# Three staging tiles, in place of two, for the output rows of an attention and SiLU layer kernel

## The chip, the cores and the metric

The kernel runs on one core of a Trainium2 chip. The metric is the device time of one execution in microseconds (us); lower is better. Beside it stands the profile of one execution. It gives the span from the first to the last instruction, every engine's instructions, and which instruction or transfer ended each wait.

## The reference, cut to what matters

The input is q, k and v with 8 batches, 8 heads, 576 positions and 64 channels. Four heads attend in a sliding window of 32 positions, the other four in a dilated window (every fourth position of 128). The result, laid out as 4608 tokens of 512 channels, goes through two dense layers with a SiLU between them:

```python
x = attn_out.transpose(0, 2, 1, 3).reshape(B * S, H * D)   # 4608 x 512
h = x @ w_in                                               # 4608 x 2048
g = h * (1.0 / (1.0 + np.exp(-h)))
out = (g @ w_out).astype(np.float32)                       # 4608 x 512
```

## The kernel before, in words

The tokens are cut into ten groups: groups 0 and 1 of 256 tokens, groups 2 to 9 of 512. For each group a first layer writes `gT` (L975 and L984 for most groups), and a second layer multiplies it by `w_out` and writes finished rows to `out`. The attention of the eight batches (score matmuls L692, exponentials L701 and L705, masks L711, products with v L738, normalisation L741 and L742) is woven between the layers' matmuls. A planner in the kernel's Python decides this order when the program is built, from its own costs and due times, and writes out one fixed order of instructions for each engine. Each engine then runs its list strictly in that order. The planner knows nothing of the staging tiles of the output.

**The second layer.** Groups 0 and 1 use `layer2`: for each block of 128 tokens ScalarE copies a finished 128x512 result out of PSUM into a staging tile `ob` (L1138) and issues its write to HBM from its own queue (L1139). Groups 2 to 9 use `layer2_fast`, which computes two blocks of 128 tokens at once with seven half-size products in place of eight. One call of it for a group has two such pairs (`tb` = 0 and 1), and a pair has two staging tiles, `ob_{g}_{tb}_0` and `ob_{g}_{tb}_1`, 128x512 in float32 each. The seven steps of a pair, n = 0 to 6, each have 8 matmuls (L1209):

- n = 0, 1 and 2: ScalarE copies the half-width result to a temporary in the buffers called `nat` (L1229).
- n = 3: VectorE adds a temporary and writes one half of the first staging tile (L1236).
- n = 4: VectorE writes one half of the second staging tile (L1236).
- n = 5: VectorE writes the other half of the first staging tile, which is then written to HBM (L1241).
- n = 6: ScalarE copies the other half of the second staging tile (L1239), which is then written to HBM (L1241).

Steps 0, 2, 4 and 6 use one PSUM bank, steps 1, 3 and 5 a second. So the matmuls of n = 5 wait until VectorE has read what n = 3 left, and those of n = 6 until VectorE has read what n = 4 left:

```python
if n > 4:
    (nc.sync if g >= BYSP else nc.scalar).dma_start(out=out[row : row + P], in_=ob)
```

The writes of groups 2 to 6 are issued from ScalarE's queue, those of groups 7 to 9 (`BYSP = 7`) from SP's.

**The staging tiles.** They come from the pool `o32`, which has two buffers for each tag. The tag `ob` thus has two, the tag `th` (results of a tanh in the first groups) has two others. Tiles take the buffers of a tag in turn. The first instruction that writes into a buffer waits until the HBM write of the tile that had the buffer before has landed. Counted through the program, the tiles are number 0 to 3 (groups 0 and 1) and then four for each group, so `ob_3_1_0` and `ob_3_1_1` are tiles 10 and 11, `ob_4_0_0` and `ob_4_0_1` are 12 and 13, `ob_4_1_0` and `ob_4_1_1` are 14 and 15, and `ob_5_0_0` and `ob_5_0_1` are 16 and 17. With two buffers tile k waits for the write of tile k - 2.

Of the kernel before, what the change touches and what calls it, by code (L numbers as in the profile page):

```python
# [10 lines left out]
F32 = mybir.dt.float32  # L11
# [5 lines left out]
def kernel(  # L17
# [11 lines left out]
    DM, DFF = moe_w_in.shape  # L29
    P = 128  # L30
# [41 lines left out]
    cpool = ctx.enter_context(tc.tile_pool(name="const", bufs=1))  # L72
    gtp = ctx.enter_context(tc.tile_pool(name="gtp", bufs=2))
    o32 = ctx.enter_context(tc.tile_pool(name="o32", bufs=2))
    dram = ctx.enter_context(tc.tile_pool(name="dram", bufs=1, space=bass.MemoryType.DRAM))
    ps_h = ctx.enter_context(tc.tile_pool(name="ps_h", bufs=2, space=bass.MemoryType.PSUM))
    ps_y = ctx.enter_context(tc.tile_pool(name="ps_y", bufs=1, space=bass.MemoryType.PSUM))
# [1042 lines left out]
    def layer2(g, l1s):  # L1120
        t0 = GROUPS[g][0]
        tiles = {}

        def l2(ring, tb, f4):
            if f4 == 0:
                tiles[tb] = POOLS[ring].tile([P, DM], F32, tag=ring, name=f"y_{g}_{tb}")
            y = tiles[tb]
            for f in range(4 * f4, 4 * f4 + 4):
                nc.tensor.matmul(  # L1129
                    y, gTs[g][:, f, tb * P : (tb + 1) * P], w_out16[:, f],  # L1130
                    start=(f == 0), stop=(f == NFF - 1),
                )
            if f4 < NFF // 4 - 1:
                return
            rows = out[t0 + tb * P : t0 + (tb + 1) * P]
            ob = o32.tile([P, DM], F32, tag="ob", name=f"ob_{g}_{tb}")
            yield "ACT", 0.12 + DM / 1200
            nc.scalar.copy(ob, y)  # L1138
            nc.scalar.dma_start(out=rows, in_=ob)  # L1139

        steps = []
        for tb in range(GROUPS[g][1] // P):
            four = [
                Step(
                    lambda ring, tb=tb, f4=f4: l2(ring, tb, f4), 0.8633, [],
                    l1s[4 * f4 : 4 * f4 + 4] + [AT_WOUT[f4]], ("ACT",) if f4 == 3 else (),
                )
                for f4 in range(NFF // 4)
            ]
            four[0].keep = four[-1]  # L1150
            four[0].rings = ["y", "u"]
            steps += four
        return steps
# [25 lines left out]
    def g_parts(g):  # L1179
        t = halves(gTs[g])  # L1180
        q = [[t[:, k, :, m * HT : (m + 1) * HT] for k in range(2)] for m in range(2)]
        u = works[(g + 1) % 2].rearrange("p (i c w) -> p i c w", i=3, c=KP)
        return q, [u[:, i] for i in range(3)]

    def g_sums(g, c):
        ((A11, A12), (A21, A22)), (S1, S2, S4) = g_parts(g)
        if g in ONPOOL:
            for args in ((S1, A21, A22, ALU.add), (S2, S1, A11), (S4, A12, S2), (A21, A11, A21)):
                yield "POOL", 0.2 + (c[1] - c[0]) * HT / 480
                minus(c, *args, eng=nc.gpsimd)  # L1190
            return
        yield "DVE", 2 * sum_us(c)
        minus(c, S1, A21, A22, ALU.add)
        minus(c, A21, A11, A21)
        yield "DVE", 2 * sum_us(c)
        minus(c, S2, S1, A11)
        minus(c, S4, A12, S2)

    def layer2_fast(g, even, odd, sums, n):
        t0 = GROUPS[g][0]  # L1200
        pq = {}
        obs = {}

        def product(bank, name, lhs, rhs, tb, first):
            if name:
                pq[bank] = POOLS[bank].tile([P, DM], F32, tag=bank, name=name)
            y = pq[bank][:, :DH]
            for c in range(KP):
                nc.tensor.matmul(  # L1209
                    y, lhs[:, c, tb * P : (tb + 1) * P], rhs[:, c],  # L1210
                    start=first and c == 0, stop=c == KP - 1, skip_group_check=not first,
                )
            return y

        def step(ring, tb, n, bank):
            ((A11, A12), (S3, A22)), (S1, S2, S4) = g_parts(g)
            t1, t5, u2 = temps
            name = f"y{n}_{g}_{tb}" if n < 2 else None
            lhs, rhs, first = (
                (A11, B11, True), (S1, T1, True), (S2, T2, False), (S4, B22, False),  # L1220
                (S3, B12, False), (A12, B21, True), (A22, T4, False),
            )[n]
            y = product(bank, name, lhs, rhs, tb, first)
            if n == 3:
                for m in range(2):
                    obs[tb, m] = o32.tile([P, DM], F32, tag="ob", name=f"ob_{g}_{tb}_{m}")
            if n < 3:
                yield "ACT", 0.13 + DH / 1200
                nc.scalar.copy((t1, t5, u2)[n], y)  # L1229
                return  # L1230
            row = t0 + tb * P + HT * (n in (4, 6))
            ob = obs[tb, int(n in (4, 6))]
            half = ob[:, DH:] if n in (3, 4) else ob[:, :DH]
            if n < 6:
                yield "DVE", 0.15 + DH / 960
                nc.vector.tensor_tensor(half, y, (u2, t5, t1)[n - 3], ALU.add)  # L1236
            else:
                yield "ACT", 0.13 + DH / 1200
                nc.scalar.copy(half, y)  # L1239
            if n > 4:  # L1240
                (nc.sync if g >= BYSP else nc.scalar).dma_start(out=out[row : row + P], in_=ob)  # L1241

        steps = []
        w3 = [w_steps["last", c] for c in WPARTS]
        w2 = [w_steps["sums", c] for c in WPARTS]
        k0, k1 = sum(even, []), sum(odd, [])
        for tb in range(HT // P):
            p_bank, q_bank = "yu" if (n + tb) % 2 == 0 else "uy"
            seven = []
            more = (k0, sums + w2, sums, sums, sums + w3, k1, k1)  # L1250
            after = ((), (), (0,), (1,), (2,), (3,), (4,))
            for i in range(7):
                bank = q_bank if i in (1, 3, 5) else p_bank
                seven.append(
                    Step(
                        lambda ring, tb=tb, i=i, bank=bank: step(ring, tb, i, bank), 0.878, [],
                        list(more[i]) + [seven[x] for x in after[i]],
                        ("DVE",) if i in (3, 4, 5) else ("ACT",),
                    )
                )  # L1260
            seven[0].keep, seven[1].keep = seven[6], seven[5]
            seven[0].rings, seven[1].rings = [p_bank], [q_bank]
            steps += seven
        return steps
# [25 lines left out]
    for g in range(FAST, NG):  # L1290
        own = [
            Step(
                lambda ring, g=g, c=c: g_sums(g, c), 0.0, (),
# [125 lines left out]
```

## Time and profile before

| | |
|---|---|
| time, median of 3 runs | 305.23 us (304.96 to 305.46) |
| the profiled execution: time | 305.17 us |
| its span | 303.4 us |
| mean granted clock of TensorE | 0.989 |
| TensorE matmul busy | 288.5 us (95% of the span) |
| VectorE, ScalarE, GpSimd busy | 215.2, 194.6, 97.9 us |
| HBM writes of staging tiles, ScalarE's queue | 24 of 256 KB, median 4.0 us from issue to landing |
| the same, SP's queue | 12 of 256 KB, median 2.0 us |

In a row of the timeline the first number is the start in us from the span's start, the second the length of the merged row, then come the engine, the line, the operation, and in brackets the engine's idle time before it with what ended it. PE is TensorE's matmul part, DVE VectorE, ACT ScalarE, POOL GpSimd, SP the engine that only issues transfers. Ends of matmuls are modelled: a matmul's successor may start before its end. The length of a merged row reaches from the first start to the last end, so that it may hold a stall.

### The profile page before, as it was taken

The numbers are of one execution on the slowest core, as the hardware profiler recorded it, in microseconds if no ns is written. First come the engines' busy times: TensorE is split into PE (matmuls) and PEld (weight loads), VectorE is DVE, ScalarE is ACT, GpSimd is POOL, SyncE is SP. The second block draws the span as 40 slices with busy tenths as digits, with TensorE's granted clock in tenths as the row PEclk, the third lists the DMA queues.
The fourth block names the chain that finished last, engine by engine and source line by source line (L and its number), as shares of the span: only waits on it lengthen the run. The fifth ranks groups of instructions, "written<-read, shape, count | busy, mean of one in ns | idle before, by whom it ended". The sixth has DMA issues, their size and how long they took to land.

```text
span 303.4 us, 7434 instructions
## 1 busy us (share of the span) xinstructions
PE 288.5 (95%) x2922; PEld 203.0 (67%) x2922; DVE 215.2 (71%) x598; ACT 194.6 (64%) x427; POOL 97.9 (32%) x135
## 2 busy tenths in 40 slices
PE   6779999989999999999989999999999999999995
PEld 2458765644567666666765577558647888888884
DVE  6288999889958785768654788476767686599511
ACT  7477784378687766766746675667665496388320
POOL 8764824000740060005000659700700069800000
PEclk9599999999999999999999999999999999999999
DMA  7999999999899989989958999943114401200231
GB/s 97 180 199 198 197 194 201 208 186 194 94 155 171 240 101 182 214 179 118 210 128 182 158 192 264 211 84 110 47 34 108 110 2 50 90 2 0 86 124 71
DMA packets 100106, 42.26 MB, mean 139 GB/s; under 512 B 68584, under 2 KB 95464, under 8 KB 100072
## 3 DMA queue, kind: packets, MB, share of 16 engines
q0 software_dynamic: 48528, 19.86, 54.2%
q1 hardware_dynamic: 48088, 15.64, 26.0%
q10 hardware_dynamic: 3456, 6.29, 6.2%
q8 instruction: 23, 0.38, 0.5%
q14 instruction: 11, 0.09, 0.1%
HBM read 39.81 MB, written 17.10 MB: 188 GB/s over the span
## 4 chain that ended last, share of the span: by engine, by line
PE 77%; DVE 11%; DMA 6%; ACT 3%; issue 1%; POOL 1%; ACTq 0%; DVEq 0%; POOLq 0%
PE h L975 27%; PE y L1209 27%; PE h L1077 8%; PE y L1129 4%; DMA out_dram<-ob 4%; PE av_d L738 2%; PE s L692 2%; DMA nat<-in_q_dram 2%; DVE gT L989 2%; PE av_p L738 1%; DVE probs L711 1%; DVE oD L742 1%; DVE ob L1236 1%; DVE oP L742 1%; PE xp L784 1%
## 5 line engine op out<-in xcount | busy, mean ns | idle before, releaser
L975 PE MATMUL h<-xA,w_in 128*128 128x512 f16 (+1 forms) x512 | 110.4, 352 | 1.8 <-ACT probs L705 0.9
L984 ACT ACTIVATE gT<-h 128x512 f16<-128x512 f32 x84 | 49.6, 597 | 29.0 <-PE h L975 28.6
L975 PEld LDWEIGHTS <-w_in 128*128 128x128 f16 x512 | 45.2, 97 | 32.6 <-issue 2.5
L1209 PEld LDWEIGHTS <-gT 128*128 128x128 f16 x512 | 49.0, 98 | 8.6 <-issue 1.6
L1209 PE MATMUL y<-w_out,gT 128*128 128x256 f16 x384 | 48.4, 273 | 0.1
L1209 PEld LDWEIGHTS <-work 128*128 128x128 f16 x384 | 37.0, 98 | 7.0 <-issue 1.1
L1236 DVE TENSOR_TENSOR ob<-y,nat 128x256 f32<-128x256 f32 x48 | 20.1, 422 | 25.4 <-PE y L1209 23.3
L512 POOL COPY fence<-kqT 128x1 f16<-128x1 f16 x10 | 3.9, 397 | 94.8 <-DMA kqT<-kq_s 94.8
L1209 PE MATMUL y<-w_sum,work 128*128 128x256 f16 x256 | 32.0, 273 | 0.4 <-ACT nat L1229 0.4
L738 PEld LDWEIGHTS <-probs 128*128 128x128 f16 x448 | 22.9, 98 | 13.0 <-DVE oP L742 1.7
L701 ACT ACTIVATE probs<-s 128x768 f16<-128x768 f32 (+2 forms) x31 | 24.5, 791 | 6.3 <-PE s L692 3.4
L742 DVE TENSOR_TENSOR oD<-av_d,rcps 72x256 f16<-72x256 f32 x64 | 26.9, 421 | 2.2
L1229 ACT COPY nat<-y 128x256 f32<-128x256 f32 x48 | 17.9, 384 | 10.7 <-PE y L1209 9.5
L987 ACT ACTIVATE th<-h 128x256 f32<-128x256 f32 (+1 forms) x44 | 19.2, 445 | 7.3 <-PE h L975 4.7
L989 DVE SCALAR_TENSOR_TENSOR gT<-th,h 128x256 f16<-128x256 f32 (+1 forms) x44 | 20.6, 487 | 2.2 <-ACT th L987 2.1
L741 DVE RECIPROCAL rcps<-av_d 72x4 f32<-72x4 f32 x64 | 11.1, 173 | 14.9 <-PE av_d L738 14.8
L1239 ACT COPY ob<-y 128x256 f32<-128x256 f32 x16 | 5.9, 371 | 24.2 <-PE y L1209 21.6
L705 ACT ACTIVATE probs<-s 128x288 f16<-128x288 f32 (+2 forms) x40 | 18.5, 485 | 4.6 <-ACT ob L1239 1.4
L742 DVE TENSOR_TENSOR oP<-av_p,rcps 96x256 f16<-96x256 f32 x48 | 20.2, 421 | 1.6
L711 DVE TENSOR_TENSOR probs<-probs,mask_p 128x768 f16<-128x768 f16 x21 | 12.2, 584 | 10.2 <-ACT probs L701 7.4
L1209 PE MATMUL y<-w_sum,gT 128*128 128x256 f16 x128 | 16.6, 272 | 1.0 <-DVE ob L1236 1.0
L738 PE MATMUL av_d<-vd,probs 128*128 128x65 f16 x256 | 16.5, 194 | 0.6 <-ACT probs L705 0.3
(129 smaller groups left out, 484.3 us busy)
## 6 DMA issues: line engine op xcount, KB each, us to landing
out_dram<-ob ACTq DMA_DIRECT2D x24, 256.0 KB, 4.0
out_dram<-ob SPq DMA_DIRECT2D x12, 256.0 KB, 2.0
kq_s<-in_k_dram POOLq DMA_DIRECT2D x5, 576.0 KB, 9.1
kq_s<-in_q_dram POOLq DMA_DIRECT2D x5, 576.0 KB, 12.9
vp<-in_v_dram POOLq DMA_DIRECT2D x7, 384.0 KB, 7.0
w_out<-in_moe_w_out_dram POOLq DMA_DIRECT2D x4, 512.0 KB, 10.9
vraw<-in_v_dram POOLq DMA_DIRECT2D x8, 224.0 KB, 5.4
w_in<-in_moe_w_in_dram POOLq DMA_DIRECT2D x3, 512.0 KB, 9.5
```

Of the source, the lines that this page charges most:

```text
L701: nc.scalar.activation(p2, both[:, :, :n], AF.Exp, scale=scale)
L705: nc.scalar.activation(p2[:, i], sp[i][:, :n], AF.Exp, scale=scale)
L738: nc.tensor.matmul(a[:, i, : D + 1], lhs(i), rhs(i), start=True, stop=True)
L742: nc.vector.tensor_tensor(o, a[:n, :, :D], rcp[:n, :, None].broadcast_to([n, HN, D]), ALU.mult)
L975: nc.tensor.matmul(h[:, :w], w_in16[:, c, f * P : (f + 1) * P], x_g[:, c], start=(c == 0), stop=(c == HP - 1),)
L984: nc.scalar.activation(gTs[g][:, f, :w], h[:, :w], AF.Silu, scale=2.0)
L987: nc.scalar.activation(th[:, :w], h[:, :w], AF.Tanh)
L989: nc.vector.scalar_tensor_tensor(gTs[g][:, f, :w], th[:, :w], 1.0, h[:, :w], ALU.add, ALU.mult)
L1077: nc.tensor.matmul(y, lhs[:, c, j], rhs[:, c], start=first and c == 0, stop=c == 1, skip_group_check=not first,)
L1209: nc.tensor.matmul(y, lhs[:, c, tb * P : (tb + 1) * P], rhs[:, c], start=first and c == 0, stop=c == KP - 1, skip_group_check=not first,)
L1229: nc.scalar.copy((t1, t5, u2)[n], y)
L1236: nc.vector.tensor_tensor(half, y, (u2, t5, t1)[n - 3], ALU.add)
```

## The change

The staging tiles get a pool of their own with three buffers, so that tile k takes the buffer of tile k - 3. The pool `o32` keeps the tag `th` and its two buffers. The lines of the kernel move down by one.

```diff
     o32 = ctx.enter_context(tc.tile_pool(name="o32", bufs=2))
+    obp = ctx.enter_context(tc.tile_pool(name="obp", bufs=3))
...
-            ob = o32.tile([P, DM], F32, tag="ob", name=f"ob_{g}_{tb}")
+            ob = obp.tile([P, DM], F32, tag="ob", name=f"ob_{g}_{tb}")
             yield "ACT", 0.12 + DM / 1200
             nc.scalar.copy(ob, y)
             nc.scalar.dma_start(out=rows, in_=ob)
...
             if n == 3:
                 for m in range(2):
-                    obs[tb, m] = o32.tile([P, DM], F32, tag="ob", name=f"ob_{g}_{tb}_{m}")
+                    obs[tb, m] = obp.tile([P, DM], F32, tag="ob", name=f"ob_{g}_{tb}_{m}")
```

In the built program every engine has the same instructions in the same order as before. The third buffer takes 2 KB in each partition behind the other two, and no other buffer has another address. What differs is which earlier write the first instructions on a staging tile wait for; VectorE has three fewer instructions that only wait (89 in place of 92), ScalarE two fewer (104 in place of 106).

## The prediction

> **What bounds the kernel now.** I read the page first. TensorE's matmuls fill 95% of the span, and the chain that ended last is mostly theirs; but the chain also has a share of a kind that no computation needs, the wait for the write of an output tile.
>
> ```profile
> PE 288.5 (95%) x2922; PEld 203.0 (67%) x2922; DVE 215.2 (71%) x598; ACT 194.6 (64%) x427; POOL 97.9 (32%) x135
> ...
> PE 77%; DVE 11%; DMA 6%; ACT 3%; issue 1%; POOL 1%; ACTq 0%; DVEq 0%; POOLq 0%
> ```
>
> The chain in order of time tells where that share lies. It passes through such a write twice, and nowhere else:
>
> ```profile
> 148.26 7.22 DMA out_dram<-ob
> 155.57 0.44 DVE ob L1236
> 156.05 1.03 PE y L1209 x8
> ...
> 178.66 5.77 DMA out_dram<-ob
> 184.56 0.43 DVE ob L1236
> 185.03 1.03 PE y L1209 x8
> ```
>
> A write in this chain does not mean that its 7.22 or 5.77 us are lost; only what an engine stood idle for it is. So the list of waits comes next, of all engines: VectorE waited twice for a write of `ob`, 1.3 us in all, and TensorE once for VectorE's step behind it.
>
> ```profile
> DVE ob L1236 <- DMA out_dram<-ob: 1.3, 2, 1.2
> ...
> PE y L1209 <- DVE ob L1236: 1.0, 1, 1.0
> ```
>
> Then the timeline of the two places. Counting the rows of L1236 in threes (n = 3, 4, 5 of a pair), the row at 155.57 is n = 4 of the first pair of group 4, which opens tile 13; the row at 184.56 is n = 3 of the first pair of group 5, which opens tile 16.
>
> ```profile
> 153.19 1.91 PE L1209 MATMUL y<-w_out,gT 128*128 128x256 f16 x16
> 153.45 0.42 DVE L1236 TENSOR_TENSOR ob<-y,nat 128x256 f32<-128x256 f32 x1 [0.53 <-PE y L1209]
> ...
> 155.57 0.42 DVE L1236 TENSOR_TENSOR ob<-y,nat 128x256 f32<-128x256 f32 x1 [1.19 <-DMA out_dram<-ob]
> ...
> 156.05 1.03 PE L1209 MATMUL y<-w_sum,gT 128*128 128x256 f16 x8 [0.95 <-DVE ob L1236]
> ```
>
> ```profile
> 183.88 2.19 PE L1209 MATMUL y<-w_out,gT 128*128 128x256 f16 x16
> ...
> 184.56 0.42 DVE L1236 TENSOR_TENSOR ob<-y,nat 128x256 f32<-128x256 f32 x1 [0.16 <-DMA out_dram<-ob]
> ```
>
> Last, the stretches behind them: how much idle time does TensorE have there that could swallow what is saved? The first figure after the stretch is its length, the second PE's busy time; the clock stands after POOL.
>
> ```profile
> 145.00:160.00 15.00, 13.86 (x166) 10.55 (x165) 9.48 (x26) 8.49 (x18) 0.00 (x0) 1.00 0.88 173
> 160.00:186.00 26.00, 25.46 (x258) 17.20 (x255) 19.14 (x48) 16.74 (x32) 13.42 (x17) 1.00 1.16 182
> 186.00:240.00 54.00, 54.00 (x485) 35.75 (x484) 35.89 (x101) 32.76 (x60) 15.20 (x23) 1.00 0.49 119
> 240.00:281.00 41.00, 40.79 (x373) 36.08 (x371) 31.60 (x84) 30.84 (x85) 18.96 (x20) 1.00 0.07 27
> ```
>
> Almost none: 0.54, 0.00 and 0.21 us. From 160 us on the kernel runs at TensorE's pace, and whatever TensorE gets earlier it keeps, unless a load is then late.
>
> **Up to the first stall** nothing changes. The instructions and their order are the same, every wait for a write names an older one, and before 154 us no instruction on a staging tile was released by a write. Durations and landings up to there are those of the trace.
>
> **The first stall, tile 13.** Before, it waits for tile 11, issued at 148.26 and landed 7.22 us later, at 155.48. After, it waits for tile 10. That write was issued at 147.42 (the row of L1241 ahead of the other), and the row at 153.45, which opened tile 12 and needed it then, was released by a matmul and not by a write; so it had landed by 153.45. VectorE is free at 155.57 - 1.19 = 154.38, so nothing holds the add back then. It takes 0.42 us to 154.80, and TensorE started 0.05 us after its end (156.05 against 155.57 + 0.43), so n = 6 may start at 154.85 or a little later. What is late next is TensorE itself: n = 4 and n = 5 started at 153.19, and 16 matmuls at 0.109 us (the chain has 1.75 us for 16 of this size) let the next one start at 154.94. TensorE gains 156.05 - 154.94 = **1.11 us**. The row's own idle time says 0.95, as it counts from the modelled end of a matmul that overlaps its successor by 0.16; I take the starts, since in an unbroken run of matmuls they set the pace, and keep 0.95 as the lower end. The margin between VectorE and TensorE is only 0.09 us, so about 0.1 could go.
>
> **Between the stalls** everything moves by 1.11 us with TensorE: the adds, the copies, the mask products and GpSimd's sums, which the waits show released by score matmuls (POOL nat L1026 by PE s, 4.0 us). TensorE has one other gap there, 0.40 us at 181.82 for a copy of ScalarE (L1229), which depends on matmuls alone and moves along.
>
> **The second stall, tile 16.** Before, it waits for tile 14 (issued 178.66, landed 184.43). After, it waits for tile 13, issued some 20 us earlier. VectorE was idle for 0.16 us, so the add starts that much earlier. TensorE started 0.05 us after the add; its own pace would have had it at 183.88 + 8 x 0.109 = 184.75, against 185.03, so 0.28 us were lost, of which 0.12 remain because VectorE came late from two masks (1.89 us for both). Gain: **0.16 us**; the ends are 0.12 (the idle time that the trace gives TensorE there) and 0.28.
>
> **What is now waited for instead.** Tile 17 (n = 4 at 186.42) waits for tile 14. It would be due at 186.42 - 1.27 = 185.15, and tile 14 landed at 184.43 even if its write, issued 1.1 us earlier, landed no earlier: 0.7 us to spare. In the later groups no wait with the two buffers was ended by a write, and tile k - 3 is always issued earlier than k - 2. Some of ScalarE's copies and issues now wait by name for a write that VectorE's wait covered before; each is an older write yet (for the issue of `ob_2_0_1` at 97.29 the write of 64.45), so nothing is held behind them. Five instructions that only wait are gone, 0.02 us each by their shortest rows, on queues that run ahead of their engines: nothing.
>
> **The sum.** 1.11 + 0.16 = 1.27 us off a span of 303.4, so 302.1; with the 1.77 us around it, 305.17 - 1.27 = 303.90 us. That execution is 0.06 us below the median of the runs, which gives 303.96, and I say **304.0 us**. With the lower ends (0.95 + 0.12) it is 304.2. The greatest gain that TensorE's idle time from 145 us to 281 us admits is 1.14 + 0.54 + 0.21 = 1.89, or 2.05 with the 0.16 of overlap: 303.2.
>
> **Rivals.** *The stall belongs to this execution.* Writes of 256 KB in the issue table land in 4.0 us on ScalarE's queue and 2.0 us on SP's in the median. If the write of tile 11 mostly took 6.1 us or less, there would be no wait at 154.38 and nothing to save: 305.2 us. Against it: the profiled execution lies within 0.3 us of all three timed runs, and none of them is a microsecond shorter. For it: landing times may vary where casts from GpSimd's queue fill the transfer engines, as they do around 148 us. The Trainium skill speaks for this rival: "DMA: Bandwidth & Descriptors", section "Anatomy of one DMA", fits a transfer as about 2.0 us plus its bytes over 436 GB/s, measured on GpSimd's path. An estimate from that page is 2.6 us for 256 KB, with which both waits would be empty and the time 305.2. The trace's 7.22 us differs, and I go by the trace. Chance 0.13.
>
> *The wait moves on to tile 17.* If tile 14 lands more than 0.7 us later than in the trace, n = 4 of group 5 waits for it. A landing 0.6 us beyond that margin would cost up to 0.6: 304.6 us. For it: 5.77 us is long already, and the transfer engines are full there. Against it: the write itself is issued earlier. Chance 0.07.
>
> *Slower: the writes come earlier and the loads land later.* Writes and loads share the transfer engines, and the loads of the next batch's k and q follow right after the writes at 156.7 and 157.6. The last transposing load for the scores at 176.03 is issued at 165.36 and lands within 3.9 us (the longest of its line), at 169.3; for those at 205.80 it is issued at 194.78 and lands by 198.7. So 6.8 and 7.1 us are to spare, 5.7 with TensorE 1.1 us earlier. The rival decides only from there: it is slower by over 0.2% when loads come 5.7 + 1.27 + 0.61 = 7.6 us later than now; 8.3 us, say, would give 305.2 - 1.3 + 2.6 = 306.5. No row shows such a delay, and no load is moved or enlarged. Chance 0.06, with whatever else a new program may bring.
>
> That the change does not do what it says is ruled out by the waits of the built program, which name the write three tiles back.
>
> **How the numbers follow.** Forecast 0.74, first rival 0.13, second 0.07, third 0.06. The forecast's own range is 303.5 to 304.5: from the sum half a microsecond to either side, which takes in the lower ends at 304.2 and the 0.25 us by which the runs scatter, and most of the way to the greatest gain. To hold eight in ten the range takes in the second rival and half of the first: 303.5 to 305.2. A measurement of this kernel can tell about 0.2%, 0.6 us, from no change. The forecast and the second rival at 304.6 are both faster by that: 0.81; the same: 0.13; slower: 0.06.
>
> **What would show it.** In the profile after: no wait of `ob` L1236 for `out_dram<-ob`; no gap of TensorE ahead of n = 6 near 155 us, which starts at about 154.9; the PE row near 183 us starting some 1.1 us earlier; the stretch 145 to 160 with about 0.2 us of idle PE in place of 1.14; no DMA `out_dram<-ob` in the chain before the end of the kernel. It would be wrong if the wait is gone and TensorE still starts n = 6 after 155.5, if PE shows a new wait of over half a microsecond after 157 us, or if the span falls by less than 0.6 us.

## The result and the profile after

The changed kernel takes 303.43 us in the median of six runs (302.88 to 303.73); the kernel before takes 305.35 us beside it (304.34 to 305.48). The ratio is 0.9941, with a 95% interval from 0.9925 to 0.9957: faster by 1.92 us. The forecast said faster, by 1.27 us; the median lies 0.07 us below the low end of its range. Three later comparisons, told below, gave less: 0.80, 1.23 and 0.82 us. Here and below a median is taken over all timed runs, while a ratio leaves out six executions that were slow as a whole: four of 308.4 to 309.9 us, one of 334.8 us (of the changed kernel) and one of 1636 us.

The profiled execution of the changed kernel took 302.88 us, with a span of 301.1 us. Busy times and the engines' shares of the chain that ended last:

```profile
PE 289.0 (96%) x2922; PEld 203.6 (68%) x2922; DVE 215.4 (72%) x598; ACT 194.7 (65%) x427; POOL 97.5 (32%) x135
...
PE 81%; DVE 9%; ACT 4%; DMA 2%; issue 1%; POOL 1%; ACTq 0%; POOLq 0%
```

The work of every engine is the same to within 0.6 us. The chain's share of DMA fell from 6% to 2%, and what is left is the first load; no write of an output tile is in it. In the waits of all engines VectorE's adds (L1237 now, one line further down) wait for matmuls and for ScalarE, above all in the two rows below; no row of this view names `out_dram<-ob`:

```profile
DVE ob L1237 <- PE y L1210: 18.5, 23, 4.0
DVE ob L1237 <- ACT nat L1230: 4.1, 1, 4.1
```

The 4.1 us behind ScalarE are not new: without the waits for writes, all idle time ahead of these adds is 23.9 us, against 23.7 before. One more of these adds, at 233.24, is put down to the transfer `x_s<-oD` with 0.63 us of idle time; the same add of the kernel before (235.45) has the same 0.63 us and there it is put down to a matmul, so nothing was added.

The timeline of the first place. Tile 13's add is the row at 153.45. It follows the mask product without a wait, and TensorE goes through n = 4, 5 and 6 without a gap:

```profile
152.33 1.91 PE L1210 MATMUL y<-w_out,gT 128*128 128x256 f16 x16
152.59 0.42 DVE L1237 TENSOR_TENSOR ob<-y,nat 128x256 f32<-128x256 f32 x1 [0.53 <-PE y L1210]
...
153.45 0.42 DVE L1237 TENSOR_TENSOR ob<-y,nat 128x256 f32<-128x256 f32 x1
154.08 1.04 PE L1210 MATMUL y<-w_sum,gT 128*128 128x256 f16 x8
```

The second place. Tile 16's add is the row at 182.34; tile 17's is the first of the two merged at 184.13:

```profile
181.91 1.94 PE L1210 MATMUL y<-w_out,gT 128*128 128x256 f16 x16
182.34 0.41 DVE L1237 TENSOR_TENSOR ob<-y,nat 128x256 f32<-128x256 f32 x1
184.13 0.74 DVE L1237 TENSOR_TENSOR ob<-y,nat 128x256 f32<-128x256 f32 x2
```

And the stretches (length first, then PE's busy time). In the first of them TensorE is now idle for 0.13 us in place of 1.14:

```profile
145.00:160.00 15.00, 14.87 (x165) 11.37 (x164) 9.52 (x27) 9.40 (x20) 0.00 (x0) 1.00 1.24 220
160.00:186.00 26.00, 25.59 (x256) 17.01 (x254) 20.57 (x52) 15.96 (x29) 15.34 (x20) 1.00 1.18 185
```

The span fell by 2.29 us, 1.02 more than forecast. Laying row on row tells why. The TensorE row ahead of the first place is already 0.86 us early (152.33 against 153.19), because the first load of q landed at 9.34 us in place of 10.07. At the first place the difference grows to 1.97 (n = 6 at 154.08 against 156.05), at the second to 2.22 (the next matmuls at 184.03 against 186.25), and then little is added. So this pair of profiles holds 1.11 us from the first place, 0.25 from the second, and 0.86 from a start whose connection with the change is open: the first question for the experiments.

### The profile page after: what moved, and what is told of

Its sections match the earlier page's. It is cut to its first block, busy times and chain, and to the rows that moved or that the text cites. A ratio compares the mean times of both kernels' runs of the same rounds, so it can differ in the third digit from the quotient of the medians.

```text
span 301.1 us, 7429 instructions
## 1 busy us (share of the span) xinstructions
PE 289.0 (96%) x2922; PEld 203.6 (68%) x2922; DVE 215.4 (72%) x598; ACT 194.7 (65%) x427; POOL 97.5 (32%) x135
## 4 chain that ended last, share of the span: by engine, by line
PE 81%; DVE 9%; ACT 4%; DMA 2%; issue 1%; POOL 1%; ACTq 0%; POOLq 0%
PE y L1210 30%; PE h L976 28%; PE h L1078 8%; PE y L1130 4%; PE s L693 3%; PE av_d L739 3%; DMA nat<-in_q_dram 2%; DVE gT L990 2%; PE av_p L739 2%; DVE probs L712 1%; ACT th L988 1%; DVE oP L743 1%; ACT probs L702 1%; PE xp L785 1%; DVE oD L743 1%
## 5 line engine op out<-in xcount | busy, mean ns | idle before, releaser
L1237 DVE TENSOR_TENSOR ob<-y,nat 128x256 f32<-128x256 f32 x48 | 20.1, 422 | 24.4 <-PE y L1210 18.5
L513 POOL COPY fence<-kqT 128x1 f16<-128x1 f16 x10 | 3.2, 329 | 93.2 <-DMA kqT<-kq_s 93.2
L1210 PE MATMUL y<-w_out,work 128*128 128x256 f16 x128 | 16.6, 273 | 0.0
```

The lines of the kernel that those rows point to most:

```text
L1210: nc.tensor.matmul(y, lhs[:, c, tb * P : (tb + 1) * P], rhs[:, c], start=first and c == 0, stop=c == KP - 1, skip_group_check=not first,)
```

## The experiments

Twelve runs were made, in three sets on three chips; some kernels were run more than once. The main theory is the prediction's: the gain comes from the waits for the writes of tiles 11 and 14, and is some 1.3 us. Against it stood that the changed program starts quicker for a reason of its own, and, as a part of rival 1, that the stalls depend on how late a write happens to land beside other transfers. In the tables below the kernel before is the one run in the same set.

**Is the result the same a second time, and does the pool matter without its third buffer?** The first kernel is the changed one; the second has the new pool with two buffers.

```diff
-    obp = ctx.enter_context(tc.tile_pool(name="obp", bufs=3))
+    obp = ctx.enter_context(tc.tile_pool(name="obp", bufs=2))
```

> The changed kernel once more. Theory 1 (the gain is the two waits of n = 4 and n = 3 for a write, 1.1 and 0.25 us, and the rest of the 1.9 us between the medians is scatter of the first loads from execution to execution): ratio to the kernel before 0.9950 to 0.9965 (1.1 to 1.5 us), and in the profile the first q load lands anywhere between 9 and 10.5 us. Theory 2 (a part of the gain, 0.5 us or more, comes from the start of the changed program, which is itself quicker): ratio 0.9935 to 0.9945, and the first q load lands near 9.3 us again.

> The pool of its own, but with two buffers as before. Theory 1: no change, within 0.2% of the kernel before (305.3 us); VectorE still idles about 1.2 us before the first add on tile 13, and TensorE starts n = 6 about 2.9 us after it started n = 4. Theory 2 (the other program is quicker at its start): 0.3 to 0.8 us faster, with the stall still there.

| | median, us | to the kernel before (304.28) |
|---|---|---|
| the changed kernel | 303.48 | 0.9967 [0.9946, 0.9987] |
| own pool, two buffers | 304.53 | 0.9991 [0.9968, 1.0014] |

The changed kernel's own time was reproduced within 0.05 us. The kernel before was quicker here than in the first comparison (304.28 against 305.35), so the gain is 0.80 us, below the 1.1 to 1.5 us expected. A pool of its own without the third buffer brings nothing that can be told from zero. Its timeline, however, isn't that of the kernel before. The wait is as large, but it stands one tile earlier: tile 12's add (154.75) waits for the write of tile 10, and tile 13's (155.61) waits for nothing:

```profile
153.21 1.04 PE L1210 MATMUL y<-w_out,gT 128*128 128x256 f16 x8
154.75 0.42 DVE L1237 TENSOR_TENSOR ob<-y,nat 128x256 f32<-128x256 f32 x1 [1.82 <-DMA out_dram<-ob]
...
155.23 1.03 PE L1210 MATMUL y<-w_out,gT 128*128 128x256 f16 x8 [0.99 <-DVE ob L1237]
...
155.61 0.42 DVE L1237 TENSOR_TENSOR ob<-y,nat 128x256 f32<-128x256 f32 x1
```

**Which tile's wait is worth what?** Two kernels keep two buffers in `o32` and give one tile a buffer of its own: tile 13, or tile 16.

```diff
+    obx = ctx.enter_context(tc.tile_pool(name="obx", bufs=1))
...
-                    obs[tb, m] = o32.tile([P, DM], F32, tag="ob", name=f"ob_{g}_{tb}_{m}")
+                    pool = obx if (g, tb, m) == (4, 0, 1) else o32    # the other: (5, 0, 0)
+                    obs[tb, m] = pool.tile([P, DM], F32, tag="ob", name=f"ob_{g}_{tb}_{m}")
```

> Two buffers as before, and a third that tile 13 alone (the second tile of group 4's first pair) takes. Theory 1: 1.1 us faster than before, 304.2 us; no gap of TensorE at n = 6 of that pair, while the add on tile 16 still waits for a write. Theory 2: 1.6 us faster, 303.7 us. A rival to both, that the wait only moves to another tile: less than 0.5 us faster.

> Two buffers as before, and a third that tile 16 alone (the first tile of group 5's first pair) takes. Theory 1: 0.25 us faster than before, 305.0 us, less than this comparison tells from none; the gap of 1.2 us on VectorE before tile 13 is still there, and the add on tile 16 starts without a wait. Theory 2: 0.8 us faster, 304.5 us.

Tile 13 alone: 304.44 us, 0.9998 [0.9979, 1.0017]. Tile 16 alone: 304.55 us, 0.9999 [0.9974, 1.0024]. Neither gains anything that these comparisons can tell from zero. For tile 13 that speaks against the forecast, whose largest term, 1.11 us, stood on this one tile. The profiled execution of that kernel took 1636 us, with TensorE busy for all but 5 of them, and shows nothing of the waits. A second profile of the same kernel does:

> The kernel with a third buffer for tile 13 alone again, for its profile. Theory 1: tile 12 (first add of group 4's first pair) now waits 1 to 1.8 us for the write of tile 10, and tile 13 then starts with no wait of its own; n = 6 starts about 2.9 us after n = 4 as before, and the time is that of before. If tile 10's write lands within 5 us instead, as in the profile of before, n = 6 starts 1.75 us after n = 4.

```profile
154.62 0.42 DVE L1238 TENSOR_TENSOR ob<-y,nat 128x256 f32<-128x256 f32 x1 [1.63 <-DMA out_dram<-ob]
...
155.48 0.42 DVE L1238 TENSOR_TENSOR ob<-y,nat 128x256 f32<-128x256 f32 x1
```

Tile 13 has no wait, and tile 12, which has no third buffer, waits 1.63 us for the write of tile 10. The kernel for tile 16 shows the same wait at tile 12 (1.97 us), and at tile 16 what the second term of the sum asked for, an add without a wait:

```profile
184.33 0.41 DVE L1238 TENSOR_TENSOR ob<-y,nat 128x256 f32<-128x256 f32 x1
```

The four profiles so far of kernels that leave tile 12 with two buffers, other than the first one, all agree: tile 10's write took 6.6 to 7.1 us and tile 12 waited 1.6 to 2.0 us for it. The profile that the prediction read, with 4.05 us for tile 10 and the wait at tile 13, is the one that differs.

**So is it tile 12?** One kernel gives tile 12 alone the third buffer (tile 13 then takes tile 10's, as in the changed kernel). A second one keeps two buffers and leaves out the writes of tiles 10 and 11 (256 rows of the output stay unwritten), so that there is nothing to wait for at the first pair. A third is the changed kernel.

```diff
-                    obs[tb, m] = o32.tile([P, DM], F32, tag="ob", name=f"ob_{g}_{tb}_{m}")
+                    pool = obx if (g, tb, m) == (4, 0, 0) else o32
+                    obs[tb, m] = pool.tile([P, DM], F32, tag="ob", name=f"ob_{g}_{tb}_{m}")
```

```diff
-            if n > 4:
+            if n > 4 and (g, tb) != (3, 1):
```

> Two buffers, and a third that tile 12 alone takes, so that tile 13 takes the buffer of tile 10; the waits of group 4's first pair are then those of the changed kernel, all others nearly those of before. Theory 1 (the gain is at this pair; the writes of tiles 10 and 11 land 4 to 7 us after their issue, and whichever of them is late is waited for, so that relieving tile 13 alone leaves the wait to tile 12): 1.0 to 1.2 us faster than before, n = 6 starts 1.7 to 1.9 us after n = 4, the wait before tile 16 is still there. Theory 2 (a part of the gain is in the start of the changed program): 0.3 to 0.5 us faster here, or 1.6 with the start. Rival to both (relieving one pair moves the wait to the next, as with tile 13 alone): no change.

> Two buffers as before; the writes to HBM of the two tiles of group 3's second pair (tiles 10 and 11, 256 rows of the output) are left out. Theory 1: the same gain as with a buffer for tile 12, 1.0 to 1.2 us, from the other side: nothing has to land. VectorE's adds on tiles 12 and 13 start without a wait for a write. If the gap had to do with the buffers or the adds themselves, it would stay, and the time with it.

> The changed kernel a third time, beside the others of this call. Theory 1: 1.0 to 1.5 us faster than before (ratio 0.9950 to 0.9967), about 0.25 us faster than the one with a buffer for tile 12 alone; its first matmul of the first layer starts at 22.0 to 23.4 us as in the other kernels. Theory 2: its first layer starts by 22.7 us once more, where kernels with two buffers start it at 23.0 or later, and it is 0.7 us or more faster than the one with a buffer for tile 12 alone.

| | median, us | to the kernel before (304.74) |
|---|---|---|
| third buffer for tile 12 alone | 304.20 | 0.9979 [0.9957, 1.0002] |
| writes of tiles 10 and 11 left out | 304.24 | 0.9981 [0.9956, 1.0006] |
| the changed kernel | 303.51 | 0.9951 [0.9929, 0.9974] |

Both reliefs of the first pair were expected to bring 1.0 to 1.2 us. They take less than half of the gain, 0.5 us of 1.23, and their intervals just reach 1; the changed kernel is 0.69 us quicker than the one with tile 12 alone, where 0.25 was expected. Their timelines show that the first place itself is repaired: n = 6 starts 1.75 us after n = 4 in both, as in the changed kernel, against 2.7 to 3.1 us with the wait. The rest is given back 30 us later, where a wait stands that the kernel before doesn't show. The first two rows are of the kernel with tile 12 relieved, the last of the one without the writes:

```profile
154.01 0.42 DVE L1238 TENSOR_TENSOR ob<-y,nat 128x256 f32<-128x256 f32 x1
...
185.78 0.76 DVE L1238 TENSOR_TENSOR ob<-y,nat 128x256 f32<-128x256 f32 x2 [0.70 <-DMA out_dram<-ob]
```

```profile
186.34 0.76 DVE L1236 TENSOR_TENSOR ob<-y,nat 128x256 f32<-128x256 f32 x2 [1.19 <-DMA out_dram<-ob]
```

These rows open tile 17, which with two buffers waits for the write of tile 15. In the chain of the first kernel that write is the row `178.08 7.61`: it was issued 1.4 us earlier than in the kernel before (179.50), and it landed at 185.69. In the kernel before, tile 17's add stood at 186.42 and found the write done. TensorE's gain moves the add to earlier than the write's landing. A small form of this wait, 0.29 us, also stands in the first profile of the pool of its own with two buffers, where nothing was relieved.

**Are the four tiles all of it?** Two buffers, and the third for tiles 12 and 16 only. Then tile 13 waits for tile 10 and tile 17 for tile 14, as in the changed kernel; tile 12 waits for none and tile 16 for tile 12, which is older than what they wait for there. Tiles 14 and 18 also wait for the one three back, all others for the one two back.

```diff
+                    pool = obx if (g, tb, m) in ((4, 0, 0), (5, 0, 0)) else o32
```

> Two buffers, and a third that only tiles 12 and 16 take, so that 13 takes the buffer of 10 and 17 that of 14, as in the changed kernel; all other tiles alternate between two buffers. Theory 1 (the whole gain lies in the waits of tiles 12, 13, 16 and 17, and relieving the first pair alone let tile 17 wait 0.4 to 1 us for the write of tile 15): the same time as the changed kernel of this call within 0.2% (303.5 us), no wait of a staging tile for a write, and 112 to 113 us and no more from the first add on tile 16 to the end of the last add but one. Theory 2 (third buffers elsewhere, or the start of the changed program, matter too): at least 0.5 us slower than the changed kernel.

> The changed kernel a fourth time. Theory 1: 1.2 to 1.5 us faster than before by the medians; its first layer starts anywhere between 22 and 23.5 us. Theory 2: its first layer starts before 23.0 us again, while kernels with two buffers stay above.

> The pool of its own with two buffers once more, for its start. Theory 1: the time of before, and a start of the first layer between 22 and 23.7 us, in the same spread as the changed kernel's. Theory 2: a start at 23.0 us or later.

| | median, us | to the kernel before (304.29) |
|---|---|---|
| third buffer for tiles 12 and 16 | 303.59 | 0.9973 [0.9956, 0.9989] |
| the changed kernel | 303.47 | 0.9972 [0.9954, 0.9990] |
| own pool, two buffers | 304.93 | 1.0017 [0.9987, 1.0047] |

The first two differ by 0.12 us, which is nothing that these runs can tell. (The changed kernel's own gain, 0.82 us here, is below the 1.2 to 1.5 us expected of it.) In the profile of the first no row of the two places waits for a write:

```profile
154.45 0.42 DVE L1238 TENSOR_TENSOR ob<-y,nat 128x256 f32<-128x256 f32 x1
...
183.19 0.41 DVE L1238 TENSOR_TENSOR ob<-y,nat 128x256 f32<-128x256 f32 x1
...
184.97 0.74 DVE L1238 TENSOR_TENSOR ob<-y,nat 128x256 f32<-128x256 f32 x2
```

The gain lies in these four tiles. That leaves the start. The first matmul of the first layer starts between 22.04 and 23.22 us in four profiles of the changed kernel, and between 22.61 and 23.43 in five with two buffers throughout. The kernels that give single tiles a buffer start between 22.72 and 23.70, this one at 22.80. The groups overlap, and this kernel takes the changed kernel's time without an early start. So the 0.86 us of the first pair of profiles is read as scatter of the first loads. The means, 22.73 us in the four and 23.08 in the nine others, still differ by 0.35 us, which so few profiles can't tell from scatter.

To keep the start out, the table counts from the add of n = 3 in the last pair before the first place (144.37 in the kernel before) to the add of tile 14, from there to that of tile 16, and on to the end of the span. The first three columns of numbers add up to the last, within rounding.

| us | to tile 14 | to tile 16 | to the end | sum |
|---|---|---|---|---|
| two buffers, mean of three profiles | 31.15 | 8.82 | 118.89 | 158.86 |
| the changed kernel, mean of four | 30.08 | 8.56 | 118.78 | 157.42 |
| third buffer for 12 and 16 | 29.94 | 8.56 | 118.81 | 157.31 |
| for 16 alone | 31.30 | 8.57 | 119.10 | 158.97 |
| for 13 alone | 30.84 | 9.12 | 118.83 | 158.78 |
| for 12 alone | 30.31 | 8.79 | 119.31 | 158.41 |
| writes of 10 and 11 left out | 29.91 | 8.82 | 119.93 | 158.66 |
| casting copies of batch 6 left out | 29.91 | 9.09 | 119.82 | 158.82 |

The change brings 1.07 us at the first place, 0.26 at the second and 0.11 behind it, 1.44 in all. Where only the first place is relieved, 0.4 to 1.0 us comes back in the column to the end.

**Why do these writes land late?** The last kernel leaves out the casting copies from HBM to HBM, on GpSimd's queue, that bring k and q of batch 6 into the form that the transposing loads read (batch 6 is computed with the k and q of batch 5).

```diff
+    kq_s[6] = kq_s[5]
...
     def issue_cast(b):
+        if b == 6:
+            return
```

> Two buffers as before; the casting copies of q and k for batch 6 (1.15 MB read, issued near 139 and 140 us) are left out, and batch 6 computes with the q and k of batch 5. Theory 1a (the writes of tiles 10 and 11 land late because those copies fill the transfer engines until 151 us): both land within 4.5 us, tiles 12 and 13 wait for nothing, n = 6 starts 1.75 us after n = 4, and with tile 17's wait for 15 taking its share the time is 0.4 to 1.0 us below before. Theory 1b (the transposing loads on SP's queue, which then come earlier, are what delays the writes): the writes still take 6 to 7 us, the wait stays, and the time is that of before within 0.2%.

The transfers between 147 and 153 us, by queue (packets, MB, share of 16 engines' time; q10 carries the writes, q0 the casting copies, q1 the transposing loads; the last number of the row of `out_dram` is the time from issue to landing). With two buffers in a pool of their own:

```profile
q1 hardware_dynamic: 2265, 0.58, 102.7%
q0 software_dynamic: 203, 0.19, 19.8%
q10 hardware_dynamic: 24, 0.05, 6.3%
...
out_dram<-ob ACTq DMA_DIRECT2D x2, 256.0 KB, 6.9
```

Without the casting copies:

```profile
q10 hardware_dynamic: 288, 0.52, 23.5%
...
out_dram<-ob ACTq DMA_DIRECT2D x2, 256.0 KB, 2.0
```

The write lands in 2.03 us instead of 4 to 7, and tiles 12 and 13 wait for nothing. So the company of other transfers makes it late. The edit takes away two neighbours at once: the transposing load that waits for the casting copies also leaves this stretch (it is issued at 131.06 in place of 145 to 151 us), so that this run doesn't tell which of the two holds the write up. A profile of the changed kernel tells more. There the casting copies came later, and between the issue of tile 10's write (146.62) and its landing (152.80) no packet of a transposing load moved, but 963 packets of GpSimd's queue did, which carried these casting copies and, until 148.05, a load of v. The write took 6.18 us: the traffic of that queue alone is enough to make it late. Whether a transposing load alone would be is not shown.

The order of the issues seems to be the rule for which tile waits, but isn't. In the four other two-buffer profiles the transposing load was issued 1.0 to 1.6 us ahead of tile 10's write, which then took 6.6 to 7.1 us. In the one that the prediction read it was issued 0.07 us behind (147.49 against 147.42): tile 10's write got through in 4.05 us, and tile 11's, issued 0.84 us later, took 7.22. Yet in two profiles of the changed kernel the write was issued 4.54 and 2.79 us ahead of the transposing load, and still took 6.18 and 6.20 us. Full transfer engines are not the whole reason either. In the own-pool profile of the rows above, only 50 packets moved between 149.3 and 150.3 us, and none of them belonged to the write that had been issued at 147.78; its first packet moved after 151.3. What holds a write back in such company, and with it which tile waits, stays open.

The time didn't follow. It was expected 0.4 to 1.0 us below the kernel before, and the median is 305.32 us, 1.0043 [1.0012, 1.0075]: slower, by a little. In the profile the second place explains why nothing is gained:

```profile
153.27 0.42 DVE L1239 TENSOR_TENSOR ob<-y,nat 128x256 f32<-128x256 f32 x1
...
185.91 0.75 DVE L1239 TENSOR_TENSOR ob<-y,nat 128x256 f32<-128x256 f32 x2 [1.32 <-DMA out_dram<-ob]
```

Tile 16 waits 0.45 us and tile 17 another 1.32, which is the wait of the other kernels that relieve the first pair alone; the sum of the table is 158.82, beside the 158.86 of two buffers. That the timed runs lie higher still, with three of the ten in the ratio between 307.4 and 308.1 us, isn't explained by this trace, and stays open.

## Why the prediction was right, point by point

**What bounds the kernel.** Right: the writes stand in the chain of the two-buffer profiles and not in that of the changed kernel, and relieving four tiles brings the whole gain, to 0.12 us in the medians.

**Up to the first stall nothing changes.** The instructions and the start, yes. But "durations and landings up to there are those of the trace" is a step that failed. Tile 10's write took 4.05 us in the trace that the prediction read, and 5.0 to 6.2 us in four profiles of the changed kernel.

**The first stall.** The size held: TensorE's n = 4 to n = 6 went from 2.86 to 1.75 us, 1.11 us, and over all profiles 1.07. The tile did not: tile 13's wait is one form of it, tile 12's the commoner, and a third buffer removes both, since tile 12 then waits for tile 9 and tile 13 for tile 10. The forecast's price was safe because either wait costs TensorE about the same (0.9 to 1.3 us over five profiles), not because it knew which; in this the number was lucky. And "nothing holds the add back" had less room than it seemed. The read trace gave tile 13 2.9 us (tile 10 landed at 151.47, VectorE was free at 154.38); the changed kernel's four profiles give 0.65, 0.43, 1.48 and 0.57 us, for instance a landing at 152.80 and the add at 153.45.

**The second stall.** Forecast 0.16, ends 0.12 to 0.28; measured 0.25 in the pair of profiles and 0.26 over all. The mis-sized step is "VectorE came late from two masks", taken with the masks' whole 1.89 us. The add starts at 182.34, 0.09 us before the modelled end of the masks (180.54 + 1.89 = 182.43). The upper end allowed for it, the value taken did not.

**Tile 17.** Forecast: 0.7 us to spare. In the changed kernel's profile tile 14's write landed at 183.01, and tile 17's add is at 184.13: 1.1 us, and 1.5 to 1.8 us in the three other profiles of it. The second rival's wait did not come, but its mechanism is real: with two buffers behind a repaired first pair tile 17 waits 0.70 to 1.32 us, for tile 15. The third buffer pays for itself twice there, and the prediction counted the second payment as nothing, because the kernel before shows no wait at tile 17.

**The sum.** Span and medians must be told apart. By profiles the change brings 1.07 + 0.26 + 0.11 = 1.44 us, against a forecast of 1.27. By medians it brings 1.92, 0.80, 1.23 and 0.82 us in four comparisons. The changed kernel is steady in them (303.43, 303.48, 303.51, 303.47); the kernel before is not (305.35, 304.28, 304.74, 304.29). The forecast subtracted from one execution at 305.17 us and so treated a number that varies by over a microsecond as fixed. Its 304.0 is 0.6 us too high, of which the sum's shortfall is 0.17 (1.44 - 1.27). The rest, about 0.4, no profile accounts for. The level of the kernel before doesn't explain it in this comparison, where its median, 305.35, lay above the 305.23 that the forecast started from. In the three later ones it lay 0.5 to 1 us below, and the gain came out smaller than the profiles'. The two-buffer executions that were profiled, at 304.81 to 305.26 us, are above those medians (304.28 to 304.74), so that 1.44 us may be the gain of the slower half of the executions. That a forecast of 1.27 lies amid 0.80 to 1.92 is in part luck.

**Rival 1, that the stall belongs to the execution.** Half right. The stall varies, both in its tile and, by the timed runs, in its size: runs of the kernel before reach down to 303.1, 303.2 and 303.5 us, the changed kernel's level. No profile caught such an execution, so that they have no stall is argued, not shown. But the stall is common enough to keep the medians apart in all four comparisons.

The 2.6 us that the prediction estimated from the Trainium skill ("DMA: Bandwidth & Descriptors", section "Anatomy of one DMA") is 0.6 us above what the write takes undisturbed, 2.03 us. Beside casting copies and transposing loads it takes 4 to 9 us, and the trace was the better source for this case.

**Rival 3, loads that land later.** Not seen: between 186 and 281 us TensorE has no gap but the 0.2 us of the first matmul of the kernel's L1078 at 263.18, which the kernel before has as well (265.42). In two of the four profiles of the changed kernel the casting copies of batch 6 did land later, at 155.3 and 155.4 us in place of 150.8, and TensorE did not wait for what follows from them.

## What to carry to other kernels

A wait for a write in one profile shows that the number of staging buffers is too small for the worst landing; which tile pays may change with the next execution, so remedy the rotation and not the tile, and take the level to subtract from several executions. Relieving one wait makes the engines arrive earlier at the next one, while a landing that is held up by other transfers doesn't come earlier with them: look one and two tiles further for writes that finish just in time, and count them as part of what the relief needs. Price the landing of a write by the transfers that share its stretch.

## What the runs showed of the hardware

The same write of 256 KB took 2.03 us with no other queue at work and up to 9.0 us in company: that one was issued at 114.63 us in the changed kernel, and while it was under way only GpSimd's queue moved packets beside the writes' own (3260 against 281). Between 147 and 153 us 24 packets of the two writes moved while the transposing load moved 2265. Landings in such company hardly follow their issue: tile 15's write was issued at 178.08, 178.14 and 177.35 us in three kernels and landed at 185.69, 186.24 and 185.81. VectorE's rows overlap a little: an add started 0.09 us before the end that the profile gives the row ahead of it, which at a stall of 0.2 us is not small.
